# Decode block with cached attention on one core: values with P stationary in chunks between the folds, wide queries, a chunked output projection and overlapped last weight columns

## The chip, the cores and the metric

The kernel runs on one core of a Trainium2 chip. A core has TensorE (PE, with its weight loads shown apart as PEld), VectorE (DVE), ScalarE (ACT), GpSimd (POOL), SyncE (SP) and 16 DMA engines. The metric is the device time in microseconds of one execution, as the median over runs.

## The reference, cut to what matters

One token (D = 640) goes through an attention block over a cache and then a gated feed-forward block, each with a layer norm in front and a residual behind it. There are 32 heads of 128, each with its own 4096 cached keys and values; all tensors are bfloat16.

```python
h  = x + A(layernorm(x))          # A: attention
    q = (x @ wq)                               # [1, 32 * 128]
    p = softmax(q . k_cache * 128**-0.5)       # per head, over 4096 keys
    o = p @ v_cache                            # per head, [1, 128]
    return o.reshape(1, 4096) @ wo             # [1, 640]
h2 = h + B(layernorm(h))          # B: feed-forward, Df = 1728
    return (gelu(x @ w_gate) * (x @ w_up)) @ w_down
```

The inputs are about 84 MB, nearly all of it the two caches (33.6 MB each); each byte is read once.

## The kernel before

**Groups.** The heads are worked in 8 groups of 4 (`HG = 4`). A group's keys form one 4 MB tile `kbuf` of 128 partitions (4 heads x 32 key blocks) x 128 rows (`r`) x 128 elements; the values form `vbuf` in the same layout. There are two buffers of each. In the text, a group is counted from 0 to 7, and K7 or V7 is the load of the last.

**Scores of a group** (`scores`, four steps of 32 rows). DVE multiplies 32 rows of K with the query, which lies broadcast over the partitions in `qb` (L296, `prod`, three buffers). PE then folds each product, with the identity as its stationary operand: eight matmuls of 512 columns add the 128 elements down to 16 (L305, into the PSUM banks `pf`, two of them). DVE reduces the 16 that are left (L312, `sc`). In the order of DVE the reduce of a step stands behind the multiply of the next.

**Query** (`query`, L281). Twenty matmuls of 128 columns per group put x @ wq of each head on that head's 32 partitions, and one ACT cast writes `qb` (L285). It is issued two groups ahead on PE, between the scores and the softmax of the group before.

**Softmax** (`softmax`). DVE takes the maximum per partition (L329), PE moves it into one row (L331, `pm`), DVE takes it per head (L334, `mrow`), PE spreads it (L337), and ACT scales it (L340, `nb`) and makes four exponentials (L344) into `P4`, a tile that holds zeros but for each head's own partitions, with the row sums in `RS`.

**Values** (`values`, L351). 128 matmuls per group: the 128x128 block of V of one row is the stationary operand, the 4 columns of `P4` of that row are the moving one, and all add into 4 columns of the PSUM bank `po`. They stand on PE behind the softmax of the following group.

**After the last group.** The sums of all heads are inverted (L370, L372), `po` is scaled (L407, `aT`), turned and spread by PE (L408 to L415) into `aP`, and 160 one-column matmuls project with `wo` (L422, every fifth column of a row block is the stationary operand). Then the residual and layer norm (L426, L248 to L265), 70 one-column matmuls each for `w_gate` and `w_up` (L454; 5 row blocks x 14 column blocks, of which the last has 64 columns), the gelu, and 56 matmuls for `w_down` (L477). A cast (L481) and the store end the kernel.

**Order.** There is no planner: `Sched` records instructions engine by engine in the order in which the Python code calls it, with the semaphore waits of each, and an engine works its list in that order. All large loads go through SP's queue in this order: wq, K0, K1, V0, then K and V in turn (K from L222, V from L231, each waiting until the group that used the buffer two groups before is done: the last multiply for K, the last values matmul for V), then V7 in three pieces, `wo` in four (they reuse the space of wq and wait for the last query), `wg` and `wu` in two each, and `w_down` in five (L395, L400). The weights of the feed-forward reuse the K and V buffers.

## Time and profile before

| | |
|---|---|
| Median of 3 runs | 206.31 us (206.18 to 206.42) |
| The profiled execution's own time | 206.16 us |
| Its span, first to last instruction | 204.9 us |
| Mean granted PE clock | 0.802 |
| PE, DVE, ACT busy | 132.3, 103.4, 24.4 us |
| DMA mean rate, HBM bytes read | 412 GB/s, 84.23 MB |
| Folds (L305), 256 matmuls | 73.9 us busy, 447 ns each |
| Values (L351), 1024 matmuls | 27.9 us busy, 165 ns each |
| Multiplies (L296), 32 | 72.4 us busy, 2282 ns each |
| Instruction packets (q8) | 14 |

The profile is of one execution. Times count from the start of the span. PE instructions overlap, so the mean duration of a small matmul is far longer than its distance from the next. `PEclk` is the share of the TensorE clock that was granted, and a window's line gives the same for a stretch. In an instruction's line the bracket tells how long its engine was idle before it and what ended that; "issue" is idle time with no wait that the profile shows.

### The profile page before, as it was taken

The page shows a single profiled execution, that of the slowest core. Times are in us where ns is not written, and L with a number is a line of the kernel's source. Part 1 is how long each engine was busy: PE and PEld are TensorE (multiplying, and loading weights), DVE is VectorE, ACT ScalarE, POOL GpSimd, SP SyncE. Part 2 cuts the span into 40 slices and gives each one's busy share as a digit, 9 for nine tenths or more (in the row PEclk, how much of TensorE's full clock was granted, in tenths as well). Part 3 has the DMA queues.
Part 4 walks back from the last instruction along what each step waited for, and adds up shares of the span by engine and source line. Part 5 has one row for each costly group of instructions (what it writes and reads, how often), then busy time and mean ns, then how long its engine had stood idle before and what let it go on. Part 6 is the DMA issues. An engine that isn't in the chain of part 4 may idle for free.

```text
span 204.9 us, 3982 instructions
## 1 busy us (share of the span) xinstructions
PE 132.3 (65%) x1847; PEld 77.5 (38%) x1847; DVE 103.4 (50%) x118; ACT 24.4 (12%) x86; POOL 2.2 (1%) x11
## 2 busy tenths in 40 slices
PE   0003057656897668785968478858776958676884
PEld 0002012222562363254326223713272228676672
DVE  2003088699579537935772777187627950101120
ACT  2001000040230040022005000500040004000000
POOL 3000000000000000000000000000000000000000
PEclk9999999999979955995799579757975797555555
DMA  7999999999999999999999999999999999999991
GB/s 256 432 432 409 416 486 422 416 416 457 448 413 416 429 453 429 416 419 440 435 435 422 413 441 448 419 419 429 441 448 419 400 413 431 429 402 421 405 358 62
DMA packets 4712, 84.48 MB, mean 412 GB/s; under 512 B 664, under 2 KB 856, under 8 KB 1880
## 3 DMA queue, kind: packets, MB, share of 16 engines
q1 hardware_dynamic: 4552, 84.23, 96.8%
q8 instruction: 14, 0.23, 0.5%
q10 hardware_dynamic: 144, 0.00, 0.0%
q14 instruction: 2, 0.02, 0.0%
HBM read 84.23 MB, written 0.00 MB: 411 GB/s over the span
## 4 chain that ended last, share of the span: by engine, by line
DMA 61%; DVE 20%; PE 13%; SPq 4%; issue 1%
DMA kbuf<-in_A_k_cache_dram 50%; DVE prod L296 16%; DMA wd_sb<-in_B_w_down_dram 10%; PE pf L305 10%; SPq L400 4%; DVE sc L312 4%; PE po L351 2%; PE pm L331 0%; PE pf L477 0%; DVE mx L329 0%; PE pz L370 0%; PE pm L337 0%; SPq L212 0%; DVE mrow L334 0%; DVE o_sb L481 0%
## 5 line engine op out<-in xcount | busy, mean ns | idle before, releaser
L305 PE MATMUL pf<-prod,Ibf 128*128 128x512 bf16 x256 | 73.9, 447 | 36.8 <-DVE prod L296 36.7
L296 DVE TENSOR_TENSOR prod<-kbuf,qb 128x4096 bf16<-128x4096 bf16 x32 | 72.4, 2282 | 27.5 <-DMA kbuf<-in_A_k_cache_dram 26.9
L305 PEld LDWEIGHTS pf<-prod,Ibf 128*128 128x128 bf16 x256 | 26.5, 111 | 81.1 <-DVE prod L296 45.9
L312 DVE TENSOR_REDUCE sc<-pf 128x32 f32<-128x512 f32 x32 | 21.9, 686 | 21.6 <-PE pf L305 21.6
L351 PE MATMUL po<-P,vbuf 128*128 128x4 bf16 x1024 | 27.9, 165 | 1.6 <-issue 1.6
L351 PEld LDWEIGHTS po<-P,vbuf 128*128 128x128 bf16 x1024 | 27.4, 100 | 1.8 <-issue 1.7
L344 ACT ACTIVATE P<-sc,nb 32x128 bf16<-32x128 f32 x32 | 18.6, 580 | 0.9
L285 ACT CAST qb<-pq 128x128 bf16<-128x128 f32 x8 | 2.1, 265 | 103.4 <-PE pq L281 103.4
L251 PE MATMUL pz<-st,ones 128*128 128x2 f32 x4 | 1.2, 364 | 17.5 <-DVE st L250 17.5
L422 PE MATMUL pf<-aP,wo_sb 128*128 128x1 bf16 x160 | 7.0, 179 | 2.3 <-issue 1.8
L344 ACT ACTIVATION_READ_ACCUMULATOR P<-sc,nb 32x1 f32 x32 | 8.1, 253 | 0.0
L422 PEld LDWEIGHTS pf<-aP,wo_sb 128*128 128x128 bf16 x160 | 6.7, 131 | 2.6 <-issue 2.0
L251 PEld LDWEIGHTS pz<-st,ones 128*128 128x128 f32 x4 | 1.0, 313 | 17.6 <-DVE st L250 17.6
L268 DVE CAST x<-x_sb 128x5 f32<-128x5 bf16 x1 | 0.2, 171 | 13.9 <-DMA x_sb<-in_A_x_dram 13.9
L281 PE MATMUL pq<-wq_sb,xb 128*32 128x128 bf16 x160 | 5.7, 232 | 1.7 <-DVE xb L265 1.7
L331 PE MATMUL pm<-I,mx 128*1 128x128 f32 x16 | 3.0, 271 | 4.6 <-DVE mx L329 4.6
L281 PEld LDWEIGHTS pq<-wq_sb,xb 128*32 128x32 bf16 x160 | 4.2, 100 | 4.8 <-issue 3.0
L337 PE MATMUL pm<-mrow,ones 1*128 1x4 f32 x16 | 3.0, 258 | 3.0 <-DVE mrow L334 3.0
L426 DVE TENSOR_TENSOR h<-x,pf 128x5 f32<-128x5 f32 x1 | 0.2, 161 | 9.1 <-PE pf L422 9.1
L262 ACT ACTIVATE ln<-ln 128x1 f32<-128x1 f32 x2 | 0.4, 202 | 35.0 <-DVE ln L260 35.0
L340 ACT ACTIVATE nb<-pm 128x4 f32<-128x4 f32 x8 | 1.4, 173 | 26.5 <-PE pm L337 26.5
L337 PEld LDWEIGHTS pm<-mrow,ones 1*128 1x128 f32 x16 | 2.3, 182 | 5.3 <-DVE mrow L334 5.3
(59 smaller groups left out, 38.2 us busy)
## 6 DMA issues: line engine op xcount, KB each, us to landing
kbuf<-in_A_k_cache_dram SPq DMA_DIRECT2D x8, 4096.0 KB, 27.1
vbuf<-in_A_v_cache_dram SPq DMA_DIRECT2D x7, 4096.0 KB, 29.3
wq_sb<-in_A_wq_dram SPq DMA_DIRECT2D x1, 5120.0 KB, 15.2
wo_sb<-in_A_wo_dram SPq DMA_DIRECT2D x2, 1920.0 KB, 26.6
vbuf<-in_A_v_cache_dram SPq DMA_DIRECT2D x1, 2048.0 KB, 16.0
vbuf<-in_A_v_cache_dram SPq DMA_DIRECT2D x1, 1536.0 KB, 19.3
wg_sb<-in_B_w_gate_dram SPq DMA_DIRECT2D x1, 1296.0 KB, 32.5
wu_sb<-in_B_w_up_dram SPq DMA_DIRECT2D x1, 1296.0 KB, 30.1
```

Of the source, the lines that this page charges most:

```text
L251: c = S.op("tensor", lambda t: t.matmul(ps[:, 0:2], ones[:, :], st[:, o:o + 2], start=True, stop=True), [b, t_one])
L281: tok = S.op("tensor", lambda t, hh=hh, c=c, n0=n0: t.matmul(pq[hh * PPH:(hh + 1) * PPH, 0:DH], xb[:, c, :], wq_sb[:, c, n0:n0 + DH], star ...
L285: t_qb[g] = S.op("scalar", lambda a: a.copy(qb[:, g, :], pq[:, 0:DH]), [tok])
L296: return S.op("vector", lambda v: v.tensor_tensor(out=prod[n % NPR][:, :, :], in0=kbuf[g % 2][:, s * RP:(s + 1) * RP, :], in1=qb[:, g, :]. ...
L305: fold_done[n] = S.op("tensor", lambda t, j=j: t.matmul(pf[n % 2][:, :], Ibf[:, :], prod[n % NPR][:, :, j * W:(j + 1) * W], start=(j == 0) ...
L312: red_done[n] = S.op("vector", lambda v: v.reduce_sum(sc[g % 2][:, s * RP:(s + 1) * RP], pf[n % 2][:, :].rearrange("p (r w) -> p r w", r=R ...
L331: b = S.op("tensor", lambda t: t.matmul(pm[0:1, 0:128], mx[:, g:g + 1], I32[:, :], start=True, stop=True), [a, t_i32, t_exp[g - 1] if g el ...
L337: d = S.op("tensor", lambda t: t.matmul(pm[:, 256:256 + HG], ones[0:1, :], mrow[0:1, g * HG:(g + 1) * HG], start=True, stop=True), [c])
L344: t_exp[g] = S.op("scalar", lambda a, lo=lo, hi=hi, h=h, hh=hh: a.activation(P4[g % 2][lo:hi, :, hh], sc[g % 2][lo:hi, :], ACTF.Exp, bias= ...
L351: t_pv[g] = S.op("tensor", lambda t, r=r: t.matmul(po[:, g * HG:(g + 1) * HG], vbuf[g % 2][:, r, :], P4[g % 2][:, r, :], start=(r == 0), s ...
L400: tok = S.dma("sync", "wd%d" % i, lambda s, s0=s0, n=n: s.dma_start(wd_sb[:, s0:s0 + n, :], B_w_down[128 * s0:128 * (s0 + n), :].rearrange ...
L422: b = S.op("tensor", lambda t, c=c, cc=cc, last=last: t.matmul(pp[:, cc:cc + 1], wo_sb[:, c, cc::NC_D], aP[:, c:c + 1], start=(c == 0 and ...
```

## The change

- **Values with P stationary.** For groups 0 to 6, four rows are taken at once (`VR = 4`): the stationary operand is `P4` of 4 rows x 4 heads (16 columns), the moving one is V of 4 rows (512 columns), and 32 matmuls add into a PSUM bank of 16 partitions x 512 (`pv`, the banks that gate and up use later). Only the blocks in which the row of P and the row of V agree are wanted: `extract` multiplies with a mask and reduces over the four rows on DVE, and one f32 matmul adds the row parts and puts the heads into `po`.
- **In chunks between folds.** The four steps of scores, the values of the group before and its extraction are interleaved by hand: steps 0 and 1, the extraction of two groups before, step 2, a quarter of the values, step 3, a quarter, then the softmax, then half of them. The last group keeps the old form (`values_last`).
- **Queries 512 wide.** Five matmuls of 512 columns per group with 128 stationary columns; four ACT casts take each head's part. The query of the next group is issued inside the softmax, between its two PE steps.
- **Output projection in four chunks** (`NW = 4`, 8 heads each). Row sums, scaling and the spreading into `aP` of three chunks are done beside the groups 3, 5 and 7 (by a masked multiply on DVE and one matmul), the fourth at the end. The 120 projection matmuls of three chunks stand on PE ahead of the last group's values.
- **Loads.** `wo` comes as three chunks in one load ahead of V7, and one behind it; V7 in two pieces, `wg` and `wu` in one each, `w_down` in pieces of 8, 4 and 1 column blocks besides the rest.
- **Last weight columns overlapped.** The rest block of gate and up takes the last 128 columns, 64 of which were done already, so that it has the shape of the others; `w_down`'s rest rows lie in the upper 64 partitions accordingly. The zeroing of the two banks goes.

```diff
-WD_PARTS = (6, 4, 2, 1)
+WD_PARTS = (8, 4, 1)
...
-        cuts = [0, R // 2, R - R // 8, R] if g == NG - 1 else [0, R]
+        cuts = [0, R - R // 4, R] if g == NG - 1 else [0, R]
...
     def query(g):
         tok = None
-        for hh in range(HG):
-            for c in range(NC_D):
-                ...
-                    pq[hh * PPH:(hh + 1) * PPH, 0:DH], xb[:, c, :], wq_sb[:, c, n0:n0 + DH],
-        t_qb[g] = S.op("scalar", lambda a: a.copy(qb[:, g, :], pq[:, 0:DH]), [tok])
+        for c in range(NC_D):
+            n0 = g * HG * DH
+            tok = S.op("tensor", lambda t, c=c, n0=n0: t.matmul(
+                pq[:, :], xb[:, c, :], wq_sb[:, c, n0:n0 + HG * DH],
+                start=(c == 0), stop=(c == NC_D - 1)),
+                [t_xb, d_wq, t_qb[g - 1] if g else None], token=(c == NC_D - 1))
+        for hh in range(HG):
+            lo, hi = hh * PPH, (hh + 1) * PPH
+            t_qb[g] = S.op("scalar", lambda a, lo=lo, hi=hi, hh=hh: a.copy(
+                qb[lo:hi, g, :], pq[lo:hi, hh * DH:(hh + 1) * DH]), [tok])
...
+    NV = R // VR
+
+    def values(g, lo, hi):
+        for i in range(lo, hi):
+            r = i * VR
+            last = i == NV - 1
+            t_pv[g] = S.op("tensor", lambda t, i=i, r=r, last=last: t.matmul(
+                pv[g % 2][0:VM, :], P4[g % 2][:, r:r + VR, :], vbuf[g % 2][:, r:r + VR, :],
+                start=(i == 0), stop=last),
+                [t_exp[g], d_v[g][r], t_ext[g - 2] if g >= 2 else None], token=last)
+        vfree[g] = t_pv[g]
...
+    def extract(g):
+        a = S.op("vector", lambda v: v.tensor_tensor(
+            out=xm[:, :, :], in0=pv[g % 2][0:VM, :].rearrange("p (r d) -> p r d", r=VR),
+            in1=rmask[:, :].unsqueeze(2).to_broadcast([VM, VR, DH]), op=ALU.mult), [t_pv[g], t_hsel])
+        t_ext[g] = S.op("vector", lambda v: v.reduce_sum(
+            xz[g % 2][:, :], xm[:, :, :].rearrange("p r d -> p d r"), axis=AX.X),
+            [a, t_acc[g - 2] if g >= 2 else None])
+        t_acc[g] = S.op("tensor", lambda t: t.matmul(
+            po[:, g * HG:(g + 1) * HG], xz[g % 2][:, :], hsel[:, :], start=True, stop=True), [t_ext[g]])
...
+    for g in range(-1, NG - 1):
+        n = g + 1
+        w = (g - 2) // 2 if g >= 2 and g % 2 == 0 else None
+        step(n, 0)
+        step(n, 1)
+        if w is not None:
+            total(w)
+        if g >= 1:
+            extract(g - 1)
+        step(n, 2)
+        if w is not None:
+            invert(w)
+            spread(w, [(po[:, w * HW:(w + 1) * HW], 0, HW, t_acc[g - 1])])
+        if g >= 0:
+            values(g, 0, NV // 4)
+        b = gather(w) if w is not None else None
+        step(n, 3)
+        if w is not None:
+            place(w, b)
+        if g >= 0:
+            values(g, NV // 4, NV // 2)
+        red(n, NP - 1)
+        ...
+        softmax(n, beside)      # beside: query(n + 1), between pm's two matmuls
+        ...
+        if g >= 0:
+            values(g, NV // 2, NV)
...
+    d_wo = load_wo(0, NW - 1)
+    load_v(NG - 1)
+    d_wo += load_wo(NW - 1, NW)
...
+    extract(NG - 2)
+    total(w)
+    invert(w)
+    for i in range(w):
+        project(i)
+    values_last(g)
+    spread(w, [(po[:, w * HW:w * HW + HG], 0, HG, t_acc[NG - 2]), (pq[:, 0:HG], HG, HG, t_pv[NG - 1])])
+    place(w, gather(w))
+    b = project(w)
```

More of the change, by code (lines that the diff above doesn't have):

```diff
@@ L28 @@
 NP = R // RP
+VR = 4
+VM = VR * HG
+NW = 4
+HW = H // NW
+DJ = 128 // HW
 NFT = 13
 NF = NFT + 1
-WD_PARTS = (6, 4, 2, 1)
+WD_PARTS = (8, 4, 1)
 WD_COLS = []
@@ L37 @@
 FREM = DF - NFT * 128
+FLO = 128 - FREM
 class Sched:
@@ L132, in bass_sequential_preLN__gqa_block_cached__glu_gated_geglu__decode_kernel @@
     wq_sb = over("wq_sb", arena, [128, NC_D, H * DH])
-    wo_sb = over("wo_sb", arena, [128, H, D])
+    wo_sb = over("wo_sb", arena, [128, NW, HW, D])
     wg_sb = over("wg_sb", kbuf[NG % 2], [128, NC_D, DF])
@@ L147, in bass_sequential_preLN__gqa_block_cached__glu_gated_geglu__decode_kernel @@
     rz = sb("rz", [128, H], FP32)
+    xm = sb("xm", [VM, VR, DH], FP32)
+    xz = [sb("xz%d" % i, [VM, DH], FP32) for i in range(2)]
+    rmask = sb("rmask", [VM, VR], FP32)
+    hsel = sb("hsel", [VM, HG], FP32)
     aT = sb("aT", [128, H], BF16)
-    aH = sb("aH", [H, DH], BF16)
+    aL = sb("aL", [128, HW, DJ], BF16)
     aP = sb("aP", [128, H], BF16)
+    jmask = sb("jmask", [128, DJ], BF16)
+    csel = sb("csel", [128, HW], BF16)
+    jred = sb("jred", [128, DJ], FP32)
+    cred = sb("cred", [128, HW], FP32)
     x_sb = sb("x_sb", [128, NC_D], BF16)
@@ L156, in bass_sequential_preLN__gqa_block_cached__glu_gated_geglu__decode_kernel @@
     ln = sb("ln", [128, 12], FP32)
-    xb = sb("xb", [128, NC_D, PPH], BF16)
+    xb = sb("xb", [128, NC_D, 128], BF16)
     hln = sb("hln", [128, NC_D], BF16)
@@ L175, in bass_sequential_preLN__gqa_block_cached__glu_gated_geglu__decode_kernel @@
     Ibf = sb("Ibf", [128, 128], BF16)
-    sel = sb("sel", [H, 4, 128], BF16)
     pf = [nc.alloc_psum_tensor("pf%d" % i, [128, 512], FP32) for i in range(2)]
@@ L185, in bass_sequential_preLN__gqa_block_cached__glu_gated_geglu__decode_kernel @@
     pu = nc.alloc_psum_tensor("pu", [128, 512], FP32)
+    pv = [pg, pu]
     t_one = S.op("vector", lambda v: v.memset(ones[:, :], 1.0))
@@ L191, in bass_sequential_preLN__gqa_block_cached__glu_gated_geglu__decode_kernel @@
     t_rs = S.op("vector", lambda v: v.memset(RS[:, :], 0.0))
-    t_pg = S.op("vector", lambda v: v.memset(pg[:, 0:NF], 0.0))
-    t_pu = S.op("vector", lambda v: v.memset(pu[:, 0:NF], 0.0))
     t_i32 = S.op("gpsimd", lambda g: g.affine_select(
@@ L204, in bass_sequential_preLN__gqa_block_cached__glu_gated_geglu__decode_kernel @@
         m32[:, :], I32[:, :].rearrange("p (j i) -> p i j", j=4), axis=AX.X))
-    t_sel = None
-    for j in range(4):
-        t_sel = S.op("gpsimd", lambda g, j=j: g.affine_select(
-            sel[:, j, :], ones_bf[0:H, :], pattern=[[1, 128]], compare_op=ALU.is_equal,
-            fill=0.0, base=-j, channel_multiplier=-4))
+    S.op("vector", lambda v: v.reduce_sum(
+        rmask[:, :], I32[0:VM, 0:VM].rearrange("p (j h) -> p j h", h=HG), axis=AX.X))
+    t_hsel = S.op("vector", lambda v: v.reduce_sum(
+        hsel[:, :], I32[0:VM, 0:VM].rearrange("p (j h) -> p h j", h=HG), axis=AX.X))
+    a = S.op("vector", lambda v: v.reduce_sum(
+        jred[:, :], I32[:, :].rearrange("p (j c) -> p j c", c=HW), axis=AX.X))
+    b = S.op("vector", lambda v: v.reduce_sum(
+        cred[:, :], I32[:, :].rearrange("p (j c) -> p c j", c=HW), axis=AX.X))
+    t_jm = S.op("vector", lambda v: v.tensor_copy(jmask[:, :], jred[:, :]), [a])
+    t_cs = S.op("vector", lambda v: v.tensor_copy(csel[:, :], cred[:, :]), [b])
     d_wq = S.dma("sync", "wq", lambda s: s.dma_start(
@@ L269, in bass_sequential_preLN__gqa_block_cached__glu_gated_geglu__decode_kernel @@
     t_xb = layernorm(x32, t_x32, 0, (
-        xb[:, :, :], x32[:, :].unsqueeze(2).to_broadcast([128, NC_D, PPH])), pz)
+        xb[:, :, :], x32[:, :].unsqueeze(2).to_broadcast([128, NC_D, 128])), pz)
     t_qb = [None] * NG
@@ L276, in query @@
         tok = None
-        for hh in range(HG):
-            for c in range(NC_D):
-                n0 = (g * HG + hh) * DH
-                last = hh == HG - 1 and c == NC_D - 1
-                tok = S.op("tensor", lambda t, hh=hh, c=c, n0=n0: t.matmul(
-                    pq[hh * PPH:(hh + 1) * PPH, 0:DH], xb[:, c, :], wq_sb[:, c, n0:n0 + DH],
-                    start=(c == 0), stop=(c == NC_D - 1)),
-                    [t_xb, d_wq, t_qb[g - 1] if g else None], token=last)
-        t_qb[g] = S.op("scalar", lambda a: a.copy(qb[:, g, :], pq[:, 0:DH]), [tok])
+        for c in range(NC_D):
[4 more added lines that the diff above has]
+                [t_xb, d_wq, t_qb[g - 1] if g else None], token=(c == NC_D - 1))
+        for hh in range(HG):
+            lo, hi = hh * PPH, (hh + 1) * PPH
+            t_qb[g] = S.op("scalar", lambda a, lo=lo, hi=hi, hh=hh: a.copy(
+                qb[lo:hi, g, :], pq[lo:hi, hh * DH:(hh + 1) * DH]), [tok])
         return tok
@@ L290, in bass_sequential_preLN__gqa_block_cached__glu_gated_geglu__decode_kernel @@
     t_exp, t_pv = [None] * NG, [None] * NG
+    t_ext, t_acc = [None] * NG, [None] * NG
+    t_rz, t_aP = [None] * NW, [None] * NW
+    t_zz, t_aL = [None], [None]
     n_piece = 0
@@ L315, in red, with step, softmax @@
             [fold_done[n], t_exp[g - 2] if g >= 2 else None])
-    def scores(g):
-        for s in range(NP):
-            tm = mult(g, s)
-            if s == NP - 1:
-                kfree[g] = tm
-            fold(g, s, tm)
-            if s >= 1:
-                red(g, s - 1)
-        red(g, NP - 1)
-    def softmax(g):
+    def step(g, s):
+        tm = mult(g, s)
+        if s == NP - 1:
+            kfree[g] = tm
+        fold(g, s, tm)
+        if s >= 1:
+            red(g, s - 1)
+    def softmax(g, beside):
         a = S.op("vector", lambda v: v.reduce_max(
@@ L333, in softmax @@
             [a, t_i32, t_exp[g - 1] if g else None])
+        beside()
         c = S.op("vector", lambda v: v.reduce_max(
@@ L347, in softmax @@
                 [e, t_p4[g % 2], t_rs, t_pv[g - 2] if g >= 2 else None])
-    def values(g):
+    NV = R // VR
[8 more added lines that the diff above has]
+        vfree[g] = t_pv[g]
@@ L350, in values, with values_last @@
+    def values_last(g):
         for r in range(R):
             t_pv[g] = S.op("tensor", lambda t, r=r: t.matmul(
-                po[:, g * HG:(g + 1) * HG], vbuf[g % 2][:, r, :], P4[g % 2][:, r, :],
-                start=(r == 0), stop=(r == R - 1)), [t_exp[g], d_v[g][r]], token=(r == R - 1))
-        vfree[g] = t_pv[g]
-    query(0)
-    scores(0)
-    query(1)
-    softmax(0)
-    load_k(2)
-    load_v(1)
-    for g in range(NG):
-        if g + 1 < NG:
-            scores(g + 1)
-            if g + 2 < NG:
-                t_qlast = query(g + 2)
-            softmax(g + 1)
-        if g == NG - 1:
-            z = S.op("tensor", lambda t: t.matmul(pz[:, 0:H], ones[:, :], RS[:, :], start=True, stop=True),
-                 [t_exp[NG - 1]])
-            t_rz = S.op("vector", lambda v: v.reciprocal(rz[:, :], pz[:, 0:H]), [z])
-        values(g)
-        if g + 3 < NG:
-            load_k(g + 3)
-        if g + 2 < NG:
-            load_v(g + 2)
+                pq[:, 0:HG], vbuf[g % 2][:, r, :], P4[g % 2][:, r, :],
+                start=(r == 0), stop=(r == R - 1)),
+                [t_exp[g], d_v[g][r], t_qb[NG - 1]], token=(r == R - 1))
@@ new lines, in total, with spread @@
+    def total(w):
+        t_zz[0] = S.op("tensor", lambda t: t.matmul(
+            pz[:, 0:HW], ones[:, :], RS[:, w * HW:(w + 1) * HW], start=True, stop=True),
+            [t_exp[2 * w + 1], t_aP[w - 1] if w else None])
+    def spread(w, src):
+        for ps, lo, n, tok in src:
+            h0 = w * HW + lo
+            a = S.op("vector", lambda v, ps=ps, h0=h0, n=n: v.tensor_mul(
+                aT[:, h0:h0 + n], ps, rz[:, h0:h0 + n]), [t_rz[w], tok])
+        t_aL[0] = S.op("vector", lambda v: v.tensor_tensor(
+            out=aL[:, :, :], in0=aT[:, w * HW:(w + 1) * HW].unsqueeze(2).to_broadcast([128, HW, DJ]),
+            in1=jmask[:, :].unsqueeze(1).to_broadcast([128, HW, DJ]), op=ALU.mult), [a, t_jm, t_aP[w - 1] if w else None])
@@ new lines, in gather, with place, invert, beside @@
+    def gather(w):
+        return S.op("tensor", lambda t: t.matmul(
+            pz[:, 16:16 + HW], aL[:, :, :], csel[:, :], start=True, stop=True), [t_aL[0], t_cs])
+    def place(w, b):
+        t_aP[w] = S.op("vector", lambda v: v.tensor_copy(
+            aP[:, w * HW:(w + 1) * HW], pz[:, 16:16 + HW]), [b])
+    def invert(w):
+        t_rz[w] = S.op("vector", lambda v: v.reciprocal(
+            rz[:, w * HW:(w + 1) * HW], pz[:, 0:HW]), [t_zz[0]])
+    query(0)
+    for g in range(-1, NG - 1):
[20 more added lines that the diff above has]
+        red(n, NP - 1)
+        def beside():
+            if n + 1 < NG:
+                t_q.append(query(n + 1))
+        t_q = []
+        softmax(n, beside)
+        if t_q:
+            t_qlast = t_q[0]
+        if g >= 0:
+            values(g, NV // 2, NV)
+        if n == 0:
+            load_k(2)
+            load_v(1)
+        if g >= 0:
+            if g + 3 < NG:
+                load_k(g + 3)
+            if g + 2 < NG - 1:
+                load_v(g + 2)
@@ L380, in pieces @@
+    g = NG - 1
+    w = NW - 1
     def pieces(slot, dst, src, cuts, waits):
@@ L387, in pieces, with load_wo @@
         return toks
-    d_wo = pieces("wo", wo_sb, A_wo[:, :].rearrange("(p c) n -> p c n", c=H),
-                  [0, 12, 24, 30, 32], [t_qlast])
+    def load_wo(lo, hi):
+        tok = S.dma("sync", "wo%d" % lo, lambda s: s.dma_start(
+            wo_sb[:, lo:hi, :, :].rearrange("p s c n -> p s (c n)"),
+            A_wo[:, :].rearrange("(s p c) n -> p s (c n)", s=NW, c=HW)[:, lo:hi, :]), [t_qlast])
+        return [tok] * (hi - lo)
+    d_wo = load_wo(0, NW - 1)
+    load_v(NG - 1)
+    d_wo += load_wo(NW - 1, NW)
     d_wg = pieces("wg", wg_sb, B_w_gate[:, :].rearrange("(p c) n -> p c n", c=NC_D),
-                  [0, 3, 5], [kfree[NG - 2]])
+                  [0, 5], [kfree[NG - 2]])
     d_wu = pieces("wu", wu_sb, B_w_up[:, :].rearrange("(p c) n -> p c n", c=NC_D),
-                  [0, 3, 5], [kfree[NG - 1]])
+                  [0, 5], [kfree[NG - 1]])
     d_wdr = S.dma("sync", "wdr", lambda s: s.dma_start(
-        wd_sb[0:FREM, NFT, :], B_w_down[NFT * 128:DF, :]), [vfree[NG - 2]])
+        wd_sb[FLO:128, NFT, :], B_w_down[NFT * 128:DF, :]), [vfree[NG - 2]])
     d_wd = []
@@ L404, in bass_sequential_preLN__gqa_block_cached__glu_gated_geglu__decode_kernel, with project @@
     d_wd.append(d_wdr)
-    a = S.op("vector", lambda v: v.tensor_mul(aT[:, :], po[:, 0:H], rz[:, :]), [t_rz, t_pv[NG - 1]])
-    a = S.op("tensor", lambda t: t.matmul(pm[0:H, 0:128], aT[:, :], Ibf[:, :], start=True, stop=True), [a])
-    a = S.op("vector", lambda v: v.tensor_copy(aH[:, :], pm[0:H, 0:128]), [a])
-    b = None
-    for j in range(4):
-        b = S.op("tensor", lambda t, j=j: t.matmul(
-            pq[:, 0:32], sel[:, j, :], aH[:, 32 * j:32 * j + 32], start=(j == 0), stop=(j == 3)),
-            [a, t_sel, t_qb[NG - 1]], token=(j == 3))
-    t_ap = S.op("vector", lambda v: v.tensor_copy(aP[:, :], pq[:, 0:32]), [b])
-    pp = pf[0]
-    for c in range(H):
-        for cc in range(NC_D):
-            last = c == H - 1 and cc == NC_D - 1
-            b = S.op("tensor", lambda t, c=c, cc=cc, last=last: t.matmul(
-                pp[:, cc:cc + 1], wo_sb[:, c, cc::NC_D], aP[:, c:c + 1],
-                start=(c == 0 and cc == 0), stop=last, skip_group_check=True),
-                [t_ap, d_wo[c]], token=last)
+    pp = pf[0]
+    def project(w):
+        tok = None
+        for c in range(HW):
+            for cc in range(NC_D):
+                last = w == NW - 1 and c == HW - 1 and cc == NC_D - 1
+                first = w == 0 and c == 0 and cc == 0
+                tok = S.op("tensor", lambda t, c=c, cc=cc, first=first, last=last: t.matmul(
+                    pp[:, cc:cc + 1], wo_sb[:, w, c, cc::NC_D], aP[:, w * HW + c:w * HW + c + 1],
+                    start=first, stop=last, skip_group_check=True),
+                    [t_aP[w], d_wo[w], red_done[NG * NP - 2]], token=last)
+        return tok
+    extract(NG - 2)
[7 more added lines that the diff above has]
+    b = project(w)
     t_h = S.op("vector", lambda v: v.tensor_add(h32[:, :], x32[:, :], pp[:, 0:NC_D]), [b])
@@ L441, in bass_sequential_preLN__gqa_block_cached__glu_gated_geglu__decode_kernel, with up @@
     t_hln = layernorm(h32, t_h, 2, (hln[:, :], h32[:, :]), pz, residual)
-    def up(ps, w, d_w, t0):
+    def up(ps, w, d_w):
         b = None
@@ L449, in up @@
                 last = c == NC_D - 1 and s == NF - 1
-                rows, cols = FREM, slice(NFT * 128, DF)
+                cols = slice(DF - 128, DF)
                 if s < NFT:
                     b0, n, k = WD_COLS[s]
-                    rows, cols = 128, slice(b0 + k, b0 + 128 * n, n)
-                b = S.op("tensor", lambda t, s=s, c=c, rows=rows, cols=cols, first=first, last=last: t.matmul(
-                    ps[0:rows, s:s + 1], w[:, c, cols], hln[:, c:c + 1],
-                    start=first, stop=last, skip_group_check=True), [t_hln, d_w[c], t0], token=last)
-        return b
-    t_g = up(pg, wg_sb, d_wg, t_pg)
-    t_u = up(pu, wu_sb, d_wu, t_pu)
+                    cols = slice(b0 + k, b0 + 128 * n, n)
+                b = S.op("tensor", lambda t, s=s, c=c, cols=cols, first=first, last=last: t.matmul(
+                    ps[:, s:s + 1], w[:, c, cols], hln[:, c:c + 1],
+                    start=first, stop=last, skip_group_check=True), [t_hln, d_w[c]], token=last)
+        return b
+    t_g = up(pg, wg_sb, d_wg)
+    t_u = up(pu, wu_sb, d_wu)
     a = S.op("vector", lambda v: v.tensor_copy(g_t[:, :], pg[:, 0:NF]), [t_g])
@@ L473, in bass_sequential_preLN__gqa_block_cached__glu_gated_geglu__decode_kernel @@
     for i, s in enumerate(order):
-        kk = FREM if s == NFT else 128
+        k0 = FLO if s == NFT else 0
         for j in range(4):
             last = i == NF - 1
-            b = S.op("tensor", lambda t, s=s, j=j, kk=kk, last=last: t.matmul(
-                pd[32 * j:32 * j + 1, 0:NQ], hm[0:kk, s:s + 1], wd_sb[0:kk, s, j * NQ:(j + 1) * NQ],
+            b = S.op("tensor", lambda t, s=s, j=j, k0=k0, last=last: t.matmul(
+                pd[32 * j:32 * j + 1, 0:NQ], hm[k0:128, s:s + 1], wd_sb[k0:128, s, j * NQ:(j + 1) * NQ],
                 start=False, stop=last, skip_group_check=True),
```

## The prediction

> **What bounds the kernel now.** I read the page first (engines, slices, chain), then the waits of SP's queue, the timeline of one group and of the tail, and windows.

> ```profile
> span 204.9 us, 3982 instructions
> PE 132.3 (65%) x1847; PEld 77.5 (38%) x1847; DVE 103.4 (50%) x118; ACT 24.4 (12%) x86; POOL 2.2 (1%) x11
> ...
> PEclk9999999999979955995799579757975797555555
> DMA  7999999999999999999999999999999999999991
> ...
> DMA 61%; DVE 20%; PE 13%; SPq 4%; issue 1%
> ```

> The 16 DMA engines are full from the second slice to the last but one, so the stream of 84 MB sets the end; DVE and PE appear in the chain because each load waits for a buffer. That wait is harmless:

> ```profile
> SPq L222 <- DVE prod L296: 90.1, 6, 34.3
> SPq L231 <- PE po L351: 55.2, 6, 19.0
> ```

> SP waits long, yet a K load lands 27.1 us after issue while its 4 MB take 9.7 us: 17 us of work are always queued ahead. So compute in the middle can be late by many microseconds before a DMA engine idles. One group, K landing at 75.2:

> ```profile
> 75.20 4.49 DVE L296 TENSOR_TENSOR prod<-kbuf,qb 128x4096 bf16<-128x4096 bf16 x2 [3.87 <-DMA kbuf<-in_A_k_cache_dram]
> 77.55 6.14 PE L305 MATMUL pf<-prod,Ibf 128*128 128x512 bf16 x16 [2.32 <-DVE prod L296]
> 84.13 1.90 PE L305 MATMUL pf<-prod,Ibf 128*128 128x512 bf16 x8 [0.44 <-DVE prod L296]
> 91.00 3.46 PE L351 MATMUL po<-P,vbuf 128*128 128x4 bf16 x128
> ```

> DVE idles 3.87 us for K: compute finishes a group before the next K is there. The mults that wait for a landing start at 75.20, 114.04 and 152.90 (the last K), so the pitch is 38.85/2 = 19.43 us a group. Eight folds took 1.90 us at full clock; sixteen took 6.14 starting at half clock. The clock matters, so I cut windows along its changes, folds alone (time, PE busy, PEld busy, PEclk, DMA share, GB/s):

> ```profile
> 51.95:55.36 3.41, 1.15 (x6) 0.30 (x4) 1.00 1.07 461
> 55.36:58.77 3.41, 0.27 (x2) 0.17 (x3) 1.00 1.05 452
> 58.77:62.19 3.42, 3.42 (x10) 1.23 (x9) 0.50 1.01 426
> 69.01:72.43 3.42, 0.52 (x3) 0.03 (x1) 1.00 1.05 450
> ```

> After a window with 0.27 us of folds the clock is 0.50, though PE was busy with 4-column matmuls throughout. After 0.52 us of folds and a 0.67 us query (69.01) it falls too; after 1.15 + 0.67 (51.95) it stays. So a 3.41 us stretch with less than roughly 1.2 to 1.8 us of wide matmuls costs the clock for at least the next stretch.

> The tail, where PE has its dense small matmuls:

> ```profile
> 174.92 2.96 PE L351 MATMUL po<-P,vbuf 128*128 128x4 bf16 x105 [1.60 <-issue]
> 181.25 5.58 PE L422 MATMUL pf<-aP,wo_sb 128*128 128x1 bf16 x128 [0.94 <-issue]
> 187.72 0.76 PE L422 MATMUL pf<-aP,wo_sb 128*128 128x1 bf16 x15 [0.89 <-issue]
> 191.26 3.71 PE L454 MATMUL pg<-hln,wg_sb 128*128 128x1 bf16 x70 [0.91 <-DVE hln L265]
> 202.87 0.32 DVE L481 CAST o_sb<-pf 128x160 bf16<-128x160 f32 x1 [3.90 <-PE pf L477]
> ```

> "issue" gaps of 1.60, 0.94 and 0.89 us come every 128 matmuls when these run dense, with nothing to wait for. Here the DMA hid them: the last cast waits for wd.

> **The change, part by part.**

> Values. Per group 128 matmuls of 4 columns go (3.46 us, 27 ns each) and 32 of 512 columns come. By the folds' row (1.90 for 8, 0.216 us apart) they cost 32 x 0.216 = 6.9 us, at half clock 13.7. So PE gains 3.4 us of work a group, or 10. [...]

> Extract (per group, on DVE between folds): a 16x512 multiply, near the 512-element reduce, 0.69 us; a reduce to 128 outputs with a strided inner axis, 0.69 at least; the two set-up reduces of I took 267 ns for 4 outputs and 369 for 32, so 124 x 3.6 ns more may come on top: 1.15. I take 0.86, together 1.55.

> Query. 20 matmuls (0.67 us) become 5 x 0.216 = 1.08, and stand behind the pm matmul, so qb is late; one cast of 265 ns becomes four, 1.05. The next group's first mult waits for them.

> So the loop from one first mult to the next, at full clock: two mults 4.45; reduce 0.61; extract 1.55; third mult 2.20 (8.8 so far); fold 1.75; eight values 1.72; last fold 1.75; eight values 1.72 (15.8); pm 0.4; query with its end 1.1; casts and handover 1.1: 18.4 us, below the 19.43 pitch by 1.0. (Before: 11.7 to the last mult's end, and the rest hidden.) The projection's chunks put 0.7 on DVE in three groups, within the 0.65 that DVE is ahead of PE there.

> Start. The first mults stood at 25.77 and 41.07; with query and casts behind pm that 15.3 becomes 17.3. The next loop lacks the extract: 16.85. So group 2's mult begins at 25.77 + 17.3 + 16.85 = 59.9, where K allowed 55.53: late by 4.4. Five loops of 18.4 bring the last group to 151.9, against K at 152.90: just in time, if the clock holds.

> Clock. Between the second fold (ended at 6.3 of the loop) and the third (8.85) PE has 2.55 us without wide work. A stretch of 3.41 that lies over it holds 0.86, under the threshold read above; by its position the clock falls in about half of the loops (0.4 to 0.7). Each fall costs a stretch at half clock on PE's chain, 1.7 us: six loops x 0.5 x 1.7 = 5.1. The last group then starts 5.1 - 1.0 = 4.1 late. [...] The window at 69.01, which was not idle and still lost the clock, speaks for my reading.

> Tail. Counted from the last group's first mult: mults, reduces, extract and spread to 12.35; fold 1.75, eight values 1.72, pm, mrow, pm 1.1 (16.9); the other sixteen values 3.5; extract 1.55, two f32 matmuls 0.9 (22.9); 120 projection matmuls at 40 ns (85 took 3.48) 4.8; the last group's values, unchanged, 3.42; two of the issue gaps, 1.9 (0 to 3.2); spread, gather, place 1.35 from the rows of L407 to L415; last 40 projections 1.75; h to hln 2.75 (188.51 to 191.26); gate and up 6.8: 140, now without the 64-row rest, with a wider column step (contiguous weights 27 ns, step 5 40 ns, so 51 at step 8 by the line through both: 6.1 by that, 7.5 as before); hm 0.33; 56 wd at 40 ns 2.25; cast to span's end 2.03. Sum 50.2, so 152.90 + 50.2 = 203.1 at the earliest. All of it is one chain on PE and DVE now: what the wo, wg and wd landings covered before is gone.

> DMA. Same bytes, V7 behind three quarters of wo, fewer and larger packets. From 199 to 202 us the DMA share was 0.64, 0.40, 0.34: engines finish apart, and 1.6 us of engine time is lost. With PE's instructions down from 1847 to about 1070 pairs, fewer of the 14 instruction packets cut into single engines. The stream may end 0 to 1.6 earlier: span 203.3 to 204.9. On SP's queue the first wo load and its wait for the last query now stand ahead of V7, whose own wait (values of group 5) ends later anyway, with 17 us queued; V7 lands near 173.7 + 9.1 = 183 (3.9 MB at 430 GB/s), before its use at 184.7. wg and wu as single loads would hold their matmuls for the whole load: at 430 GB/s wg lands near 191 and wu near 196, and PE's chain reaches them at 191.7 plus the lateness, and 3.4 later; with no lateness that is the 0.9 by which the stream may hold rival 1 back. Set-up reduces lie in the 14 us wait for x; the last wd in 4 columns before 1 instead of 2 costs up to 0.3 where DMA is last.

> **Sum.** 203.1 + 4.1 late + half a clock loss in the last group 0.85 = 208.1 span. The profiled run was 206.16 for a span of 204.9, 1.26 more, and 0.15 under the median of 206.31: 208.1 + 1.26 + 0.15 = 209.5 us.

> **The rivals.** (1) The clock holds: PE is busier than before, and from 31 to 56 us of the old kernel, with steady folds and no wait for K, the clock stayed full. Then the chain's 203.1 (204.0 where wu holds it) and the stream's 203.3 meet: 204.7 to 205.4 us, faster. It decides as long as clock losses sum below 1.0 plus the 1.6 that the stream leaves. Against it: from the twelfth slice on, every second to fourth slice of the clock's row shows a 5 or 7. Chance 0.24, less a case where a loss of some 1.7 just eats the gain (no change): 0.05.
> (2) PE becomes the bound outright: a stationary tile of 16 columns may not count as activity, as the 4-column stream did not. At half clock a group has (32 + 5 + 32) x 0.43 = 29.7 us of PE against 19.43; a third of that excess over six groups is 20 us, so 215 to 230. Chance 0.11.
> Forecast, late by a few microseconds: 0.60.

> **Numbers.** What a measurement can tell is about 0.2%, 0.4 us. Forecast's own ends: reduce 0.69 or 1.15 (seven times -0.17 or +0.29), falls in 0.4 to 0.7 of the loops (-1 to +2), gaps and weight steps (-2.5 to +2): 206.5 to 213.5. With rival 1 below and part of 2 above: 204.5 to 214.5.

> **What would show it.** Right: the last K's first mult starts 2 to 6 us after its landing; the final cast is released by PE with wd long landed; PE's chain holds the tail; DMA share falls early; fold stretches at clock 0.5 in the middle. Wrong: mults still wait for K throughout, the cast follows a wd landing, PEclk near 9 (rival 1); loops over 21 us and DMA gaps in the middle (rival 2).

## The result, and the profile after

| | before | after |
|---|---|---|
| Median (runs) | 206.33 us (206.18 to 206.64, 6) | 218.57 us (216.47 to 219.44, 6) |
| The profiled execution's own time, span | 206.16, 204.9 us | 218.09, 216.8 us |
| Instruction packets (q8) | 14 | 8 |

The ratio is 1.058, 95% interval 1.052 to 1.063. Slower was forecast, by the mechanism that the forecast named, but the span is 8.7 us above the 208.1 of its sum and the time is outside its range of 204.5 to 214.5.

The page after: span, the slices of the clock and the DMA, the chain that ended last.

```profile
span 216.8 us, 2482 instructions
...
PEclk9999999979999999889979996999699979955555
DMA  6999999999999999999999999999957999999300
...
PE 48%; DVE 34%; DMA 11%; ACT 4%; issue 2%; SPq 0%; DVEq 0%
```

DMA led the chain with 61% and is down to 11%. Its row has a hole in the two slices from 157 to 168 us and ends more than two slices early: the stream no longer sets the end, it waits. SP's queue shows for what (us in total, times, longest):

```profile
SPq L237 <- DVE prod L315: 87.5, 6, 34.4
SPq L478 <- PE pm L354: 16.7, 1, 16.7
```

K's waits on the multiplies are what they were. New is L478: the first load of `wo` stands for the last query for 16.7 us, with V7 and all later loads behind it, and that is longer than what was queued ahead. The new order did not make the hole, though: `wo` was issued at 162.74, and V7's own wait, for the values of group 5, ended 3.9 us later, at 166.60. It is the lateness of compute that held both.

The clock's row looks better than before (mean 0.89 against 0.802), and this misleads. First, the first multiplies of three groups and the third fold step of two of them, from the timeline:

```profile
62.01 4.49 DVE L315 TENSOR_TENSOR prod<-kbuf,qb 128x4096 bf16<-128x4096 bf16 x2 [2.10 <-ACT qb L300]
71.09 1.90 PE L324 MATMUL pf<-prod,Ibf 128*128 128x512 bf16 x8 [1.82 <-DVE prod L315]
81.11 4.49 DVE L315 TENSOR_TENSOR prod<-kbuf,qb 128x4096 bf16<-128x4096 bf16 x2 [2.11 <-ACT qb L300]
90.19 3.21 PE L324 MATMUL pf<-prod,Ibf 128*128 128x512 bf16 x8 [1.82 <-DVE prod L315]
101.88 4.50 DVE L315 TENSOR_TENSOR prod<-kbuf,qb 128x4096 bf16<-128x4096 bf16 x2 [2.11 <-ACT qb L300]
```

From the second group on no first multiply waits for K any more; they wait for `qb`, the casts behind the query. The loop from 62.01 takes 19.10 us, the next 20.77, with the same eight folds at 1.90 in one and 3.21 in the other. The windows, cut where the granted clock changes and counting folds alone, show why (PE busy, PEld busy, clock, DMA share, GB/s):

```profile
66.74:70.15 3.41, 1.72 (x8) 0.58 (x6) 1.00 1.05 452
...
87.21:90.63 3.42, 0.79 (x4) 0.21 (x3) 1.00 1.02 436
90.63:94.04 3.41, 2.77 (x7) 0.73 (x5) 0.50 1.04 442
107.69:111.11 3.42, 0.79 (x4) 0.21 (x3) 1.00 1.05 450
...
169.13:172.55 3.42, 1.27 (x6) 0.39 (x4) 1.00 1.01 431
172.55:175.96 3.41, 2.93 (x7) 1.04 (x8) 0.50 1.12 478
```

With 1.72 us of folds in the window the clock stays; with 0.79 to 1.27 the next window has 0.50. The first multiplies stand at 25.92, 43.46, 62.01, 81.11, 101.88, 122.62, 143.37 and 163.95; the clock falls at 46.25, 90.63, 111.11, 131.59, 152.07 and 172.55. The five from 90.63 on stand 20.48 us apart, each from the next. That is six windows of 3.413, which is how long each stretch at half clock ahead of the tail lasted, and the loop with one fall takes 20.58 to 20.77, nearly the same: once a window lay over the gap between the second and the third fold step, the sixth window after it did so again. The position does drift a little: from the loop's first multiply to the fall it is 9.52, 9.23, 8.97, 8.70 and 8.60 us, and the folds in the window before it grow from 0.79 to 1.27. Of all seven loops after the first, the last group's included, six had a fall; the one at 46.25 came behind 3.28 us in which PE was idle, the others behind at most 1.82.

The tail, on PE and DVE alone:

```profile
188.75 4.92 PE L510 MATMUL pf<-aP,wo_sb 128*128 128x1 bf16 x120
...
195.58 2.72 PE L380 MATMUL pq<-P,vbuf 128*128 128x4 bf16 x96 [1.06 <-issue]
...
202.04 0.52 PE L510 MATMUL pf<-aP,wo_sb 128*128 128x1 bf16 x10 [1.35 <-issue]
...
214.81 0.32 DVE L580 CAST o_sb<-pf 128x160 bf16<-128x160 f32 x1 [2.24 <-PE pf L576]
```

The dense small matmuls have issue gaps of 1.06 and 1.35 us, where the kernel before had 1.60, 0.94 and 0.89 and the loads hid them, and the last cast waits for PE with the last load landed 10 us earlier (204.4). From the last group's first multiply to the end it is 52.85 us.

### The profile page after: what moved, and what is told of

Read it like the earlier page. It is cut to its first block, busy times and chain, and to the rows that moved or that the text cites. A ratio compares the mean times of both kernels' runs of the same rounds, so it can differ in the third digit from the quotient of the medians.

```text
span 216.8 us, 2482 instructions
## 1 busy us (share of the span) xinstructions
PE 161.4 (74%) x1074; PEld 73.9 (34%) x1074; DVE 118.6 (55%) x149; ACT 30.4 (14%) x110; POOL 1.2 (1%) x7
## 4 chain that ended last, share of the span: by engine, by line
PE 48%; DVE 34%; DMA 11%; ACT 4%; issue 2%; SPq 0%; DVEq 0%
DVE prod L315 24%; PE pf L324 19%; DMA kbuf<-in_A_k_cache_dram 11%; PE pg L372 9%; PE pu L372 5%; PE pq L294 4%; ACT qb L300 3%; DVE xz L389 3%; DVE sc L331 3%; PE pf L510 3%; DVE xm L386 2%; PE pq L380 2%; PE pg L553 2%; PE pu L553 2%; PE pf L576 1%
## 5 line engine op out<-in xcount | busy, mean ns | idle before, releaser
L324 PE MATMUL pf<-prod,Ibf 128*128 128x512 bf16 x256 | 71.7, 433 | 23.5 <-DVE prod L315 23.0
L372 PE MATMUL pg<-vbuf,P 128*16 128x512 bf16 x128 | 30.0, 382 | 0.0
L300 ACT CAST qb<-pq 32x128 bf16<-32x128 f32 x32 | 8.2, 256 | 121.1 <-PE pq L294 120.5
L372 PE MATMUL pu<-vbuf,P 128*16 128x512 bf16 x96 | 22.3, 380 | 0.0
L361 ACT ACTIVATE P<-sc,nb 32x128 bf16<-32x128 f32 x32 | 18.4, 576 | 0.9
L372 PEld LDWEIGHTS pg<-vbuf,P 128*16 128x16 bf16 x128 | 10.6, 90 | 17.7 <-issue 4.8
L294 PE MATMUL pq<-wq_sb,xb 128*128 128x512 bf16 x40 | 11.1, 412 | 2.2 <-DVE xb L280 2.2
L372 PEld LDWEIGHTS pu<-vbuf,P 128*16 128x16 bf16 x96 | 7.9, 90 | 13.1 <-issue 3.3
L389 DVE TENSOR_REDUCE xz<-xm 16x128 f32<-16x512 f32 x7 | 7.1, 1019 | 0.2
L351 DVE TENSOR_REDUCE mrow<-pm 1x4 f32<-1x128 f32 x8 | 2.2, 278 | 7.7 <-PE pm L347 7.7
L294 PEld LDWEIGHTS pq<-wq_sb,xb 128*128 128x128 bf16 x40 | 3.4, 102 | 7.2 <-issue 2.4
L392 PE MATMUL po<-hsel,xz 16*128 16x4 f32 x14 | 2.7, 258 | 4.0 <-DVE xz L389 4.0
## 6 DMA issues: line engine op xcount, KB each, us to landing
wg_sb<-in_B_w_gate_dram SPq DMA_DIRECT2D x1, 2160.0 KB, 24.4
```

Source lines behind the costliest of these rows:

```text
L294: tok = S.op("tensor", lambda t, c=c, n0=n0: t.matmul(pq[:, :], xb[:, c, :], wq_sb[:, c, n0:n0 + HG * DH], start=(c == 0), stop=(c == NC_D ...
L300: t_qb[g] = S.op("scalar", lambda a, lo=lo, hi=hi, hh=hh: a.copy(qb[lo:hi, g, :], pq[lo:hi, hh * DH:(hh + 1) * DH]), [tok])
L324: fold_done[n] = S.op("tensor", lambda t, j=j: t.matmul(pf[n % 2][:, :], Ibf[:, :], prod[n % NPR][:, :, j * W:(j + 1) * W], start=(j == 0) ...
L361: t_exp[g] = S.op("scalar", lambda a, lo=lo, hi=hi, h=h, hh=hh: a.activation(P4[g % 2][lo:hi, :, hh], sc[g % 2][lo:hi, :], ACTF.Exp, bias= ...
L372: t_pv[g] = S.op("tensor", lambda t, i=i, r=r, last=last: t.matmul(pv[g % 2][0:VM, :], P4[g % 2][:, r:r + VR, :], vbuf[g % 2][:, r:r + VR, :],
L389: t_ext[g] = S.op("vector", lambda v: v.reduce_sum(xz[g % 2][:, :], xm[:, :, :].rearrange("p r d -> p d r"), axis=AX.X), [a, t_acc[g - 2] ...
```

## The experiments

**1. The query in the gap.** The next group's query moved from the softmax to behind the second fold step, where PE waits for DVE:

```diff
         step(n, 0)
         step(n, 1)
+        if n + 1 < NG:
+            t_qlast = query(n + 1)
...
-        softmax(n, beside)          # with query(n + 1)
+        softmax(n, lambda: None)
```

> The changed kernel with one edit: the query of the next group stands behind the second fold step instead of inside the softmax, in the stretch where PE had nothing wide to do. Theory (the loop from one group's first mult to the next is longer than the 19.4 us in which K arrives, because query and casts stand in its chain (2.4 us) and because the clock falls in the empty stretch once per loop (1.65 us)): both go, the loop's own length falls from 20.75 to about 16.7 and every first mult waits for K again, the last at about 153 instead of 163.95; the rest of the chain, 52.85 us, loses the last group's clock loss too: span 204 to 206, time 205.3 to 207.3 us. Rival (PE is simply full: 69 wide matmuls a group): the work is the same, loops stay at 20 us or more, the last first mult is later than 158 and the span over 210.

Measured: 205.81 us (10 runs, 204.88 to 206.41), ratio 0.997, interval 0.996 to 0.999; profiled span 205.0. The multiplies wait for K again from 94.64 on, and the last group starts at 152.92 instead of 163.95:

```profile
133.50 4.49 DVE L315 TENSOR_TENSOR prod<-kbuf,qb 128x4096 bf16<-128x4096 bf16 x2 [2.44 <-DMA kbuf<-in_A_k_cache_dram]
```

One move of five matmuls and four casts gives back 11.8 us of span: 11.0 in the loops, 0.8 in the tail. It does two things at once, though: it takes the query off the loop's chain, and it puts wide columns into the empty window. The next one separates them.

**2. Filling the gap with wide work.** Nothing is moved; six matmuls of 512 columns that nothing needs are added:

```diff
         step(n, 1)
+        for i in range(6):
+            S.op("tensor", lambda t: t.matmul(
+                pq[:, :], Ibf[:, :], xb[:, 0:4, :], start=True, stop=True), [t_qb[n], t_xb, t_ibf], token=False)
```

> The changed kernel with six more matmuls of 512 columns per group, whose result nobody reads, behind the second fold step: 1.3 us more of PE work per group, nothing taken away. Theory (the empty stretch costs the clock in every loop): the clock no longer falls in the third fold step, loops come to 19.1 to 19.4 us, the last first mult to about 158, the last group too keeps its clock: span 208 to 211, 6 to 9 us faster with more work. Rival (the half clock is only a sign of waiting and costs nothing, or PE is full): span unchanged at 215 to 218, or longer by up to 8 x 1.3 = 10 us.

Measured: 209.72 us (2 runs), ratio 1.017, interval 1.015 to 1.019; span 208.5. Five loops in a row take 19.09 to 19.15 us, and the clock falls only at 46.4 and in the tail. In the loop from 81.44 the gap and the third fold step are now

```profile
87.73 1.46 PE L428 MATMUL pq<-xb,Ibf 128*128 128x512 bf16 x6
...
90.54 1.90 PE L324 MATMUL pf<-prod,Ibf 128*128 128x512 bf16 x8 [0.92 <-DVE prod L315]
```

More work makes the kernel 8.9 us faster than the change. So the falls after 46 us cost some 8 us (216.8 against 208.5 of span); the loop of 19.1 is the rest.

**3. Filling it with narrow work.** The same place, 48 matmuls of 4 columns, so that PE is as busy but streams few columns:

```diff
+        for i in range(48):
+            S.op("tensor", lambda t: t.matmul(
+                pq[:, 0:4], Ibf[:, :], xb[:, 0, 0:4], start=True, stop=True), [t_qb[n], t_xb, t_ibf], token=False)
```

> The changed kernel with 48 more matmuls of only 4 columns (identity times the wide query's operand, a result that nothing reads) in the gap between second and third fold, where the other filler had six of 512 columns. At the 27 ns of the 4-column stream they take 1.3 us of the gap's 1.8 to 2.5, so PE idles for about 1 us there and no chain grows. If what keeps the clock is that PE is not idle, this works like the wide filler: last group's first mult near 158, span 208 to 209. My theory is that only columns streamed count: the stretch over the gap still holds 0.8 to 1.3 us of wide matmuls, the clock falls to 0.5 once in nearly every loop as without filler, last first mult 162 to 165, span 215 to 218.

Measured: 218.86 us (4 runs, 217.81 to 219.71), ratio 1.060, interval 1.057 to 1.064; the last group starts at 165.65, later still than the theory's 162 to 165. After a first fall at 44.70 the clock falls at 92.48, 112.96, 133.44, 153.92 and 174.40, again 20.48 from one to the next. The windows, all PE work counted (PE, PEld, DVE, ACT and POOL busy, clock):

```profile
89.07:92.48 3.41, 2.49 (x54) 1.96 (x51) 3.38 (x5) 0.00 (x0) 0.00 (x0) 1.00 1.01 432
92.48:95.90 3.42, 3.42 (x9) 0.96 (x8) 3.13 (x4) 0.00 (x0) 0.00 (x0) 0.50 0.96 412
```

PE was busy for 2.49 us of this window, its longest idle stretch was 0.92, and the clock was lost all the same; folds filled 0.82 of it. Six matmuls of 512 columns in this place (1.46 us, experiment 2) kept the clock, 48 of 4 columns did not, so a busier PE alone was not enough. Near 1.3 us of folds it is less clear: a window from 68.59 of this run, with 1.32 us of folds, kept the clock, and one from 70.71 in experiment 6, with 1.33, lost it. Whether narrow columns count a little is not shown.

**4. No extract.** The masked multiply and the strided reduce taken out, zeros in their place:

```diff
-        a = S.op("vector", ... xm ...)
-        t_ext[g] = S.op("vector", lambda v: v.reduce_sum(xz[g % 2][:, :], ...
+        t_ext[g] = t_pv[g]
```

> The changed kernel without the masked multiply and the reduce on DVE (the sums that they make are left out, zeros stand in their place; the matmul behind them stays). Theory: 1.65 us of DVE leave the loop's chain, the empty stretch on PE shrinks from 2.2 to about 0.6 us, so the clock holds too: 20.75 - 1.65 - 1.65 = 17.45 us, below 19.4, so first mults wait for K, the last at 153; the tail loses 1.65 twice and 1.7: about 47.9, so that the end of the DMA stream (204.4 in the changed kernel, some 1 to 2 us earlier without the late V7) sets the end again: span 203 to 205.5. Rival (only the extract's own time counts): loops of 19.1, last first mult near 157, span 207 to 210.

Measured: 205.03 us (2 runs), ratio 0.994, interval 0.992 to 0.996. Loops take 17.46 to 17.49 until they wait for K. Taking 1.65 us out of the gap both shortens the loop and closes the hole in the window: the clock does not fall between 46 us and the tail. The end is set by `w_up`, one load whose 70 matmuls wait for all of it (195.39) and take 3.57.

**5. The wide query in the kernel before,** at its old place, two groups ahead (the same `query` as in the change, nothing else).

> The kernel before with the wide query alone (five matmuls of 512 columns, four casts), at its old place two groups ahead. Theory (the query hurts by its place, not by its form): time within 0.4 us of the kernel before, the loads still end the kernel. Rival (the wide form itself costs, 0.4 us more PE and 0.8 us more ACT per group on the path): 1 to 3 us slower.

Measured: 206.26 us (10 runs), ratio 1.000, interval 0.999 to 1.001. The form of the query costs nothing here, where the loads end the kernel and a little more work on PE is hidden; its place in the change does cost.

**6. The values in one block.** The two quarters between the folds put behind the softmax with the rest:

```diff
-        if g >= 0:
-            values(g, 0, NV // 4)
...
-        if g >= 0:
-            values(g, NV // 4, NV // 2)
...
-            values(g, NV // 2, NV)
+            values(g, 0, NV)
```

> The changed kernel with the 32 value matmuls of a group in one block behind the softmax, instead of 8 + 8 between the folds and 16 behind. Theory: the chunks between the folds use PE time in which it would wait for DVE anyway (from third fold's end to the next mult's end), so in one block all 32 (7.3 us by 16 in 3.6) stand ahead of the next loop's first fold; a loop gets 1.5 to 3 us longer, span 219 to 226. Rival: the chunks between the folds lengthen the chain from first mult to the last reduce by their 2 x 1.85; then the block lets the scores end earlier, a loop gets up to 3.6 shorter and the span falls to 203 to 207.

Measured: 227.56 us (2 runs), ratio 1.103, interval 1.096 to 1.109; span 227.7, even above the theory's 219 to 226. The block stands ahead of the next group's folds:

```profile
103.13 7.07 PE L372 MATMUL pg<-vbuf,P 128*16 128x512 bf16 x32
...
110.14 3.63 PE L324 MATMUL pf<-prod,Ibf 128*128 128x512 bf16 x16
```

The product of 104.13 to 106.4 was folded only from 110.14. Chunks between folds are what makes the wide form bearable; the loops from 60 us on take 21.1 to 24.7 us, not near six windows, and the falls come irregularly.

**7. The old values in chunks.** Experiment 1 with 128 matmuls of 4 columns a group in the place of the wide ones, so that no extract is needed (the groups' sums in two banks by turns), with `w_up` in two loads and in one:

```diff
-            t_pv[g] = ... pv[g % 2][0:VM, :], P4[g % 2][:, r:r + VR, :], vbuf[g % 2][:, r:r + VR, :]
+            t_pv[g] = ... pv[g // 2 % 2][:, g * HG:(g + 1) * HG], vbuf[g % 2][:, r, :], P4[g % 2][:, r, :]
...
-                  [0, 5], [kfree[NG - 1]])
+                  [0, 3, 5], [kfree[NG - 1]])
```

> The kernel with the query in the gap, and the values as before (128 matmuls of 4 columns a group, written straight to the sums, so no extract), but in chunks between the folds and alternating between two banks by pairs of groups; w_up in two loads (3 and 2 blocks) as before. The loop loses the extract (1.6 us on DVE) and about 5 us of PE; the last group's first mult waits for K near 152.9, the tail behind it loses two extracts and 16 wide value matmuls, 5 to 7 us of the 52.1, so the chain reaches up before the last of w_up lands (near 195.4). The end is then set by the loads: last landing near 200.7, then the last four wd matmuls, cast and output, 2.4: span 203.0 to 203.6, 204.2 to 204.9 us, ratio 0.990 to 0.993. Rival: the clock, which 4-column matmuls do not hold, falls in every loop as in the kernel before, and PE's tail at half clock ends behind the loads: span 204.5 to 206.

> The same with w_up as one load, as in the change. All 70 of its matmuls wait for the whole of it, near 195.4, and end 3.6 later; then gelu's product, 56 wd, cast: 195.4 + 3.6 + 0.3 + 2.2 + 2.3 = 203.8 span, 204.9 to 205.2 us, 0.3 to 0.6 above the version with two loads. Rival: the last wd landing sets the end in both, no difference.

Measured: 206.33 us (11 runs), ratio 1.000, interval 0.999 to 1.001, with two loads; 206.84 us (9 runs), 1.002, interval 1.001 to 1.003, with one. The 0.5 between them is as expected; both times are above those expected. With two loads the span, 205.2, lies in the rival's range, but not for the rival's reason: PE reached `w_down` with time to spare and waited 1.15 and 0.33 us for it. The loads themselves ended late, at 202.6 and 202.8 instead of 200.7, and `w_up` as one load landed at 197.56 instead of 195.4. The two kernels have 13 instruction packets, the change and experiments 1 and 4 have 8, experiment 2 has 9. In every kernel whose loads compute did not hold up, 8 or 9 packets went with a last landing of 200.7 to 200.9, and 13 or 14 (the kernel before and experiment 5 too) with 202.5 to 202.8. That asked for a test.

**8. Few instructions, and some put back.** Experiment 1 with wide values except for group 6, whose values take the old form so that no extract stands in the tail, and `w_up` in two loads; then the same with 48 narrow matmuls more per group:

```diff
+        if g == NG - 2:
+            for r in range(lo * VR, hi * VR):
+                ...  pv[g % 2][:, 0:HG], vbuf[g % 2][:, r, :], P4[g % 2][:, r, :]
...
-    extract(NG - 2)
```

> The kernel with the query in the gap and wide values, but group 6's values as 128 matmuls of 4 columns like the last group's, so that no extract stands in the tail, and w_up in two loads (3 and 2 blocks). With few instructions (some 9 instruction packets) the loads should end near 200.7 as in the other kernels with 8 or 9, not near 202.6 as in those with 13 or 14. The tail behind the last K loses 1.8 of chunks, 1.8 behind the softmax and 2.5 of extract from 52.1, so PE comes to w_up before its landing, and the last wd landing sets the end: 200.7 + 0.3 + 0.3 + 2.0 = 203.2 span (203.0 to 203.6), 204.3 to 204.8 us, ratio 0.990 to 0.993. Rival: instruction packets do not matter, the loads end at 202.5 whenever they are not waited for: span 205.

> The same with 48 matmuls of 4 columns more in each group's gap (768 instructions over the kernel, 3 instruction packets of 16 KB, a 16th of a per cent of the bytes; 1.3 us of PE in a gap that has 1.4 left, so the scores' chain hardly moves). If instruction packets hold up single DMA engines by 1.3 to 1.5 us each, the last landing moves from about 200.7 towards 202.5 though no load has changed, and the span grows by 0.5 to 1.9. If they do not matter, last landing and span stay within 0.3 of the version without them.

Measured: 204.53 us (6 runs), ratio 0.993, interval 0.991 to 0.995; and with the narrow matmuls 206.20 us (10 runs), ratio 1.000, interval 0.999 to 1.001. The first beats both kernels. Five of its six runs lie at 204.47 to 204.71; the profiled one, 205.96, is the odd one, and its end shows where the time went. Page, last matmuls, and a window (PE, PEld, DVE, ACT, POOL busy, clock, DMA share):

```profile
q8 instruction: 9, 0.15, 0.3%
```
```profile
202.23 0.30 PE L579 MATMUL pf<-wd_sb,hm 128*1 128x160 bf16 x4 [1.12 <-DMA wd_sb<-in_B_w_down_dram]
```
```profile
200.00:202.00 2.00, 0.81 (x20) 0.36 (x16) 0.00 (x0) 0.00 (x0) 0.00 (x0) 0.50 0.02 8
```

Fifteen DMA engines were done by 200.72; one ended at 202.19, 1.47 later. In the trace the ninth instruction packet runs from 200.00 to 201.01, and the last 4 bytes of the loads move at 201.00, when all else had ended by 200.29: the window has a DMA share of 0.02, and PE still waited 1.12 us for `w_down` until 202.23, 0.04 behind the last engine. That the time of the ninth packet made this run the odd one is the author's reading of one trace. With three packets more,

```profile
q8 instruction: 12, 0.20, 0.4%
```

three engines ended at 201.9 to 202.0, the others by 200.7, and the median rose by 1.67 us with the loads unchanged. PE was not late: the last group starts at 152.72 (152.81 without the narrow matmuls), and PE stood before `w_down` at 198.64 and waited 1.16 us.

## Why the forecast was right and where it was wrong

**Right.** The old form of the values was not the dear one (128 narrow matmuls took 3.46 us, 32 wide ones 7.07 in experiment 6), the query and its casts came onto the chain from one first multiply to the next, the window over the gap lost the clock, the end went over to PE and DVE. The multiplies waited for `qb`, not K; the last cast followed PE; `wd` had long landed. All of that was forecast, and the direction. But the last group's first multiply came 10.8 us after its K had landed (153.11), where 2 to 6 were forecast.

**Wrong in four sizes.** The step that failed is "just in time, if the clock holds" with falls "in about half of the loops": the loop had too small a margin under K's pitch, and the clock fell in nearly every loop. The last group started at 163.95 where the sum had 152.90 + 4.1 = 157.0, 6.95 late; the tail took 52.85 where it had 50.2 + 0.85, 1.8 late.

- *The loop at full clock: +3.5.* "18.4 us" was 19.10. Along 62.01 to 81.11: query with its end 1.29 (for 1.1), casts and handover 1.20 (for 1.1), extract 1.65 (1.55; the strided reduce took 1.02, where 0.86 had been taken between 0.69 and 1.15), third multiply to the first fold 2.33 (2.20), the four blocks of eight 7.22 (6.94). No term is far off, but nearly all lean the same way, and five loops multiply them. They took 0.7 of the margin of 1.0 under K's pitch of 19.43, so a late group could no longer catch up.
- *The count of falls: +3.0.* "By its position the clock falls in about half of the loops" treated the position as random. A loop of 19.1 with one fall of 1.65 is 20.75, and six windows are 20.48, so the position repeated. Five of the six loops from 43.46 had a fall; they took 8.1 us more than loops without one, against 5.1. Experiment 2 takes the falls after 46 us away and gets 6.0 us back at the last group's start, the rest in the tail.
- *The start: +0.45.* The first multiply stood at 25.92 (25.77), the first loop took 17.54 (17.3), the second 18.55, of which 1.65 is a fall (16.9, forecast 16.85).
- *The tail: +1.8.* The clock fell there too (+0.8 over the half that was taken), the two issue gaps were 2.41 (1.9), the blocks and the reduce again the rest. The 120 projection matmuls took 4.92 (4.8), gate and up 6.95 (6.8), `w_down` 2.13 (2.25).

**The DMA.** "17 us always queued ahead" was right for the old order of loads. A lateness that grew to 11 us used it up: `wo` stood 16.7 us for the last query, V7 3.9 longer for its buffer, and from 160 to 162 us the DMA share was 0.21. It cost nothing, since compute ended later still. "The stream may end 0 to 1.6 earlier" was a little more than 1.6 where compute allowed it: 200.7 against 202.47. In experiment 8 three more instruction packets went with 1.67 us more of the median, with the loads unchanged; that fewer packets explain most of the 1.8 here is the author's estimate from it.

**The rivals.** The clock did not hold (1). PE did not become the bound outright (2), though one of its signs, a gap in the DMA, appeared from 157 to 168 us: the loops stayed under 21 us, and the clock was kept with a stationary tile of 16 columns and 512 moving ones. In the changed kernel the window from 100.87 to 104.28 holds 3.40 us of these and no fold, and the next one has 1.00; in experiment 6 blocks of 7.07 us of them stand in a row, and the clock stayed full from 98.0 to 139.0 us. What the change would have been with the first fall alone is near experiment 2's 208.5 of span, not rival 1's 204: that rival had the loop too short as well.

**Idle stretches of PE.** The fall at 46.25 came behind 3.28 us of idle PE, with 0.44 us of folds in the window that ends there. In the later loops no idle stretch passes 1.82 us, and the clock fell five times more; in the window of experiment 3 the longest is 0.92, and it still fell. What sets these windows apart in the traces is the wide work: 0.79 to 1.27 us of 512-column matmuls in a window of the changed kernel lost the clock, 1.72 kept it.

## What to carry to other kernels

Before a step goes onto the chain from one group to the next, see whether a wait elsewhere in the loop has room for it: five matmuls and four casts cost 11.8 us in one place, some 8 of it lost clock (216.8 against 208.5 of span in experiment 2), and nothing that the time shows in another. Count wide columns, not busy time, in each 3.41 us of PE: here a window with 1.72 us of folds kept the clock, and one with PE busy for 2.49 us, 0.82 of it folds, lost it. When a loop's length with one slow window comes near a whole number of windows, as 20.75 came near 20.48 here, price the fall in every loop. Where loads end the kernel, count the PE instructions too: 768 more of them came with three more instruction packets and 1.67 us in experiment 8.
